# Small weight copies moved between engines and new planner ranks in a four-layer attention and gated-MLP kernel on one core

## The chip, the core and the metric

The kernel runs on one core of a Trainium2 chip. The metric is the device time of one execution in microseconds (us). The engines are TensorE (PE, its weight loads PEld), VectorE (DVE), ScalarE (ACT), GpSimd (POOL) and SyncE (SP), which issues the DMAs.

## The reference

One sequence of 2048 tokens with 576 features passes four layers: attention, MLP, attention, MLP, with the same weights both times. Each layer adds its result to its input.

```python
x = A_x
x = x + _A_ref(_layernorm(x, axis=-1), A_wqkv, A_wo)
x = x + _B_ref(_layernorm(x, axis=-1), B_w_gate, B_w_up, B_w_down)
x = x + _A_ref(_layernorm(x, axis=-1), A_wqkv, A_wo)
x = x + _B_ref(_layernorm(x, axis=-1), B_w_gate, B_w_up, B_w_down)
```

`_A_ref` has 32 heads of width 18. A token attends to 8 positions: itself and the 7 that lie 2, 4, ... 14 tokens before it; positions before the start are masked. The logits are scaled by 18 ** -0.5, a softmax over the 8 follows, then the weighted sum of values and the product with `wo` (576 x 576). `_B_ref` is `((x @ w_gate) * (x @ w_up)) @ w_down` with an inner width of 4608. Inputs and output are bfloat16.

## The kernel before

**Layout and loops.** Tokens lie in tiles of 128. Features are held on partitions in five blocks (four of 128, a tail of 64). The attention runs in jobs `j`: job 0 is tile 0 alone, job 1 tile 1 alone, and each later job is a chunk of two tiles; `seq` lists them. Jobs 0 to 4 belong to the first attention layer, job 5 is the first of the second. The MLP runs as `first_pair` (tiles 0 and 1), then `small(2)`, `small(3)`, `small(4)` (a chunk each), then `big` (four tiles at a time). In a `first_pair`, `small` or `big`, gate and up columns are multiplied in units (L1046, their 64-row tails in L1056), evacuated by ScalarE and VectorE (L1000 to L1005), and the down product follows in blocks (L1100, L1101). Projection units of a later attention job are put between the gate/up units where `IN_GU` says: in `{0: {3: [2]}}` job 2 goes in before unit 3 of `first_pair`.

**Preparing the weights.** `wqkv` is loaded raw (`wraw` for query and key, `wrav` for value) and copied into another order, one block `k` of 128 rows at a time, by `permute` (L351). For each `k` there are pieces by `t3`: 0 is query and 1 is key (128 x 512 each), 3 is the small rest of query and key (128 x 128), 2 and 4 are the same for value. Before, VectorE takes queries and most keys, ScalarE the keys of blocks 1 and 4 in two halves, and POOL the small pieces of blocks 0 to 3.

**An attention job.** `head` is the layer norm: statistics (L424, L426) on VectorE, the reciprocal root on ScalarE (L430, L431), the apply step on VectorE (L448) or ScalarE (L442, L443), then a transpose, either on PE (L460) with a ScalarE copy (L463), or by DMA (L453). `attention` runs one `head` before the projection (L551, for job 0 and part of job 1 L599), and one after it (its argument `ab` is 1) for the MLP input `xnT_B`. Between them: query x key products (`l1`, L744), sums over the head width (for jobs 0 and 1 on PE with the 0/1 matrix `Esel`, L760), softmax (L785, L798, L828 or L841), spreading the weights back over the partitions (`Bsel`, L863, or a DMA), value products (L912, L928; job 0 sums them on PE, L916 and L917), `wo` (L951; job 0 L479). Job 0 (`fast`) divides by the softmax sum only at the end: `total` makes the reciprocal (L834 to L836), `spread_z` and `rzs` spread it.

**Order of the work.** Every piece is registered with `op(engine, cost, function, r=, w=, prio=, after=)`: the data that it reads and writes, an estimated cost, and a rank (1 by default). `Plan.run` then simulates and emits the instructions; each engine runs its own in that order. Among all candidates it takes

```python
key = (t, o.prio, o.idx)
```

so the earliest estimated start wins, then the lowest rank, then the place in the list. `after` adds an order without data. Two details matter at the start: the identity matrix (`mk_ident`, L315 and L316), the zeroed halos (`mk_zero`, L334 and L336) and the selection matrices (`mk_sel`, L369 to L379: `Esel`, `Bsel`, `capb`) are all POOL pieces that can start at time 0; and before each PE piece the planner adds warm-up matmuls on the identity (`warm`, L967) for the idle time that it expects:

```python
self.warm(min(44, int(max(0, t - clock["PE"] - 100) / 100)))
```

This stops with the first gate/up unit (`bb`), whose pieces are chained in a fixed order on PE. The load of tile 2 waits for a small POOL memset (L307) that reads the small piece of block 0 (`wq3_0`); all loads of `wo` and of the MLP weights are queued behind it on SP.

Of the kernel before, what the change touches and what calls it, by code (L numbers as in the profile page):

```python
# [141 lines left out]
def kernel(  # L142
# [34 lines left out]
    KACT, VENG = (1, 4), ('POOL', 'POOL', 'ACT', 'ACT', 'ACT')  # L177
# [153 lines left out]
    def setup_b():  # L331
# [6 lines left out]
        def permute(k, t3, eng, prio, d0=0, nd=16, **kw):  # L338
            if t3 < 3:
                src = (wrav[:, k, :] if t3 == 2 else wraw[:, k, t3 * D:(t3 + 1) * D]).rearrange("p (h d) -> p d h", h=H)[:, d0:d0 + nd, :]  # L340
                dst = wqkv[:, k, t3 * 512 + d0 * H:t3 * 512 + (d0 + nd) * H].rearrange("p (d h) -> p d h", h=H)
                cost = {"DVE": 50 + 35 * nd, "ACT": 60 + 64 * nd, "POOL": 200 + 106 * nd}[eng]
            else:
                a, m = (0, 2) if t3 == 3 else (2, 1)
                src = (wrav[:, k, :] if a else wraw[:, k, :]).rearrange("p (t h d) -> p t d h", t=m, h=H)[:, :, 16:18, :]
                dst = wqkv[:, k, 1536 + 64 * a:1536 + 64 * (a + m)].rearrange("p (t d h) -> p t d h", t=m, h=H)
                cost = {"DVE": 80 + 75 * m, "ACT": 160 + 130 * m, "POOL": 250 + 180 * m}[eng]
            nm = "wrav" if t3 in (2, 4) else "wraw"
            rk = [f"{nm}{k}"] if k < KF else [f"{nm}t0", f"{nm}t{TL}"]
            cp = {"DVE": nc.vector.tensor_copy, "ACT": nc.scalar.copy, "POOL": nc.gpsimd.tensor_copy}[eng]  # L350
            return op(eng, cost, lambda: cp(dst, src), r=rk, w=[f"wq{t3}_{k}" + (f"_{d0}" if nd < 16 else "")], prio=prio, **kw)  # L351
# [34 lines left out]
        op("POOL", 3200, mk_sel, w=["sel"], prio=1)  # L386
# [11 lines left out]
        op("POOL", 0, swap, r=[f"wq{t}_{k}" for t in (0, 1, 3) for k in range(KT)],  # L398
# [20 lines left out]
    def head(src, keys, nst, dst, dkeys, prio, ab, on_pe, mg, first=None, then=None, dve=False):  # L419
# [19 lines left out]
        for i in range(nst):  # L439
# [4 lines left out]
            if dve:  # L444
# [4 lines left out]
                op("DVE", 420, apply_v, r=[keys[i], *mk, f"rstd{ab}"], w=[f"xn{ab}{i}"], prio=prio)  # L449
# [71 lines left out]
    LN1P = {2: 1.5, 3: 3, 4: 2, 5: 2.5, 6: 2.5, 7: 3, 8: 1, 1: 0.4}  # L521
    ATP = {1: 3, 2: 2.5, 3: 2.5, 4: 3, 5: 3, 6: 2}
    LPP = {1: 2.5, 2: 2, 3: 2.5, 4: 1.5, 5: 1.5, 6: 2}

    def attention(j, la, t0, nst, units=None):
# [5 lines left out]
        on_pe, pe_sum = j < 4, j < 2  # L531
        prio, mg = (1, 0) if fast else (ATP.get(j, 3), 200 if j < 5 else 1500)
# [5 lines left out]
        head(lambda i: xin[:, i0 + i, :], xin_k, nst, xnT_A, xk, LN1P.get(j, prio), 0, j < 3, mg, None,marks["evq"] if j == 1 else None, j < 3)  # L538
# [41 lines left out]
        def project(tag, au, bu, tl, ea, eb, dkeys):  # L580
# [35 lines left out]
            if fast:  # L616
# [14 lines left out]
                def values():  # L631
# [9 lines left out]
                    for cost, fn, w_, eng in eb[2:]:  # L641
                        op("ACT", cost, lambda fn=fn: fn(ub, 0), r=[kb, "uv"], w=w_, prio=0.5, free="unit", use=ub)
# [95 lines left out]
        for p_ in range(W // 2):  # L738
# [27 lines left out]
            op("DVE", 60 + 5.6 * n, l1, r=qk, w=[pk], prio=lprio, after=marks["xb1"] if j == 1 and p_ == 3 else None)  # L766
# [35 lines left out]
        else:  # L802
# [20 lines left out]
            op("DVE", 100 + 7 * n, gather_l, r=[f"part{jj}" for jj in range(4)] + ["cap"], w=["Lt"], prio=prio - 1, margin=2500 if j < 5 else 3000)  # L823
            op("DVE", 240 + 4.5 * n, soft1d, w=["Lt", "mx", "rg"], prio=prio - 1)
        if fast:
            late["values"]()
            rz = xn_[1][1]
            op("ACT", 170 + 1.8 * n, lambda: nc.scalar.activation(late["a_c"][:, 0:W * sq], late["Lt"][:, 0:W * sq], ACT.Exp),  # L828
               r=["Lt"], w=["ac"], prio=0)

# [25 lines left out]
        if on_pe:  # L856
# [15 lines left out]
            if fast:  # L872
                late["total"]()
                br = Bank()

                def spread_z():
                    for e in range(4):
                        for h_ in range(2):
                            nc.tensor.matmul(br()[:, e * sq:(e + 1) * sq], lhsT=Bsel[:, e].rearrange("p a b -> p (a b)"),
                                             rhs=rz[:, h_ * sq:(h_ + 1) * sq], start=(e == 0 and h_ == 0), stop=(h_ == 1), skip_group_check=True)  # L880
                op("PE", 350, spread_z, r=["zs", "xn11", "sel"], prio=0, **br.take())
                rzs = lambda: late["Lt"][:, 2 * P:2 * P + n]
                op("ACT", 300, lambda: nc.scalar.copy(rzs(), br()[:, 0:n]), r=[br.key, "Lt"], w=["rzs"], prio=0.5, **br.drop())
# [15 lines left out]
        for i_ in range(W):  # L899
# [21 lines left out]
            if fast:  # L921
# [3 lines left out]
                else:  # L925
                    marks["sum"] = op("PE", 330, gather, r=[pvk, "ident"], w=[bo[0].key, bo[1].key], prio=0)
            elif i_:
# [35 lines left out]
        head(lambda i: xs_f[:, i0 + i, :], fk, nst, xT, xTk, (1 if j > 1 else 0.5) if j < JSM + 2 else prio - 1, 1, j < 4, mg, None, None, j < 3)  # L963
# [366 lines left out]
    IN_GU, IN_D = {0: {3: [2]}, 2: {0: [3], 7: [4]}, 3: {2: [5], 12: [6]}}, {}  # L1330
# [41 lines left out]
```

## Time and profile before

| | us |
|---|---|
| median of 3 runs | 1048.6 (1048.55 to 1049.17) |
| the profiled execution | 1048.55 |
| its span in the profile | 1046.7 |
| PE busy | 1028.5 (98% of the span) |
| DVE busy | 723.0 (69%) |
| ACT busy | 446.3 (43%) |
| POOL busy | 14.5 (1%) |

A line of a timeline gives the start in us, the duration in us, the engine, the line of the kernel, the operation, output<-inputs, shapes, and how many instructions were merged (`x44`); in brackets the idle time before it and what ended that. Lines of the chain of waits give start, duration, engine, output and line. PE's ends are modelled, so pieces overlap by about 0.17 us.

### The profile page before, as it was taken

To read this page: it belongs to the slowest core of one execution; us is meant where nothing else is said; L and a number is where in the kernel's file an instruction comes from. 1 tells how busy PE (TensorE), PEld (TensorE's weight loads), DVE (VectorE), ACT (ScalarE), POOL (GpSimd) and SP (SyncE) were. 2 spreads that over 40 slices of the span, in tenths; PEclk is the share of its full clock that TensorE was granted. 3 is DMA by queue.
4 is the path that set the end of the run, shared out by engine and by line. 5 is a ranking of instruction groups with operands and counts; after the bars stand their busy time and mean duration, and the time that the engine had idled before them with its cause. 6 is when DMAs were issued, how large, how long until landed. Compare 5 with 4: busy or idle time off the path is not lost.

```text
span 1046.7 us, 19602 instructions
## 1 busy us (share of the span) xinstructions
PE 1028.5 (98%) x7898; PEld 595.9 (57%) x8016; DVE 723.0 (69%) x1366; ACT 446.3 (43%) x905; POOL 14.5 (1%) x54
## 2 busy tenths in 40 slices
PE   7999999999999999999999999999999999999998
PEld 6886886777765445554455544564455644554444
DVE  7896797889849886396766967579684796832211
ACT  4663763554645641354424443154531444214420
POOL 5000000000000000000000000000000000000000
PEclk9999999999999999999999999999999999999999
DMA  8918117454743805455143641635435352454212
GB/s 241 327 69 194 51 41 229 109 130 149 176 123 101 227 12 147 126 158 177 48 127 94 189 133 51 160 67 181 134 85 159 100 165 85 122 152 136 68 49 88
DMA packets 139834, 135.50 MB, mean 129 GB/s; under 512 B 43360, under 2 KB 137440, under 8 KB 139744
## 3 DMA queue, kind: packets, MB, share of 16 engines
q1 hardware_dynamic: 139744, 134.25, 45.0%
q8 instruction: 62, 1.02, 0.4%
q14 instruction: 28, 0.23, 0.1%
HBM read 114.49 MB, written 10.88 MB: 120 GB/s over the span
## 4 chain that ended last, share of the span: by engine, by line
PE 96%; issue 1%; DVE 1%; POOL 1%; ACT 0%; POOLq 0%; DVEq 0%
PE pu L1046 20%; PE pg L1046 18%; PE pg L1100 9%; PE pu L1100 8%; PE acct L1046 6%; PE pg L551 5%; PE pa L1046 4%; PE pu L551 4%; PE acct L1100 3%; PE pu L1056 3%; PE pg L1056 3%; PE pa L1100 2%; PE pg L1101 2%; PE pu L1101 2%; PE pa L951 1%
## 5 line engine op out<-in xcount | busy, mean ns | idle before, releaser
L1046 PEld LDWEIGHTS <-reg 128*128 128x128 bf16 x3072 | 277.5, 98 | 222.6 <-issue 24.2
L1046 PE MATMUL pu<-xnT_B,reg 128*128 128x512 bf16 (+2 forms) x1302 | 231.4, 316 | 1.3 <-issue 0.3
L1046 PE MATMUL pg<-xnT_B,reg 128*128 128x512 bf16 (+2 forms) x1204 | 220.4, 319 | 1.0 <-issue 0.2
L1100 PEld LDWEIGHTS <-reg 128*128 128x128 bf16 x864 | 84.4, 98 | 101.5
L1000 ACT CAST g_sb<-pu 128x512 bf16<-128x512 f32 x112 | 65.5, 588 | 126.3 <-PE pg L1056 66.2
L1003 DVE TENSOR_TENSOR reg<-reg,g_sb 128x512 bf16<-128x512 bf16 x144 | 59.7, 419 | 86.2 <-ACT reg L1002 76.6
L551 PEld LDWEIGHTS <-wqkv 128*128 128x128 bf16 (+1 forms) x1050 | 88.2, 97 | 34.0 <-issue 18.2
L744 DVE TENSOR_TENSOR prod<-qT,kT 128x2560 bf16<-128x2560 bf16 (+1 forms) x68 | 95.8, 1411 | 8.2 <-ACT kT L671 7.3
L912 DVE TENSOR_TENSOR prod<-vT,ab 128x1280 bf16<-128x1280 bf16 (+1 forms) x120 | 92.1, 776 | 0.0
L1000 ACT CAST g_sb<-pg 128x512 bf16<-128x512 f32 x112 | 65.8, 589 | 60.6 <-PE pu L1056 29.9
L928 DVE TENSOR_TENSOR qT<-qT,prod 128x1280 bf16<-128x1280 bf16 (+1 forms) x112 | 89.7, 801 | 2.5
L1101 PEld LDWEIGHTS <-reg 128*128 128x128 bf16 x864 | 84.9, 98 | 1.0
L430 ACT ACTIVATE rstd<-mv,eps_t 128x2 f32<-128x2 f32 (+1 forms) x33 | 9.8, 297 | 162.8 <-DVE mv L426 159.9
L1046 PE MATMUL acct<-xnT_B,reg 128*128 128x512 bf16 (+1 forms) x303 | 69.4, 354 | 0.5 <-issue 0.3
L551 PE MATMUL pg<-xnT_A,wqkv 128*128 128x256 bf16 (+1 forms) x500 | 69.6, 273 | 0.0
L1056 PE MATMUL pu<-xnT_B,reg 64*128 64x512 bf16 (+2 forms) x331 | 67.7, 316 | 0.1
L1101 PE MATMUL pu<-wd,reg 128*128 128x64 bf16 x336 | 64.8, 193 | 0.8
L1100 PE MATMUL pg<-wd,reg 128*128 128x512 bf16 x231 | 64.5, 380 | 0.0
L1056 PE MATMUL pg<-xnT_B,reg 64*128 64x512 bf16 (+2 forms) x305 | 62.8, 319 | 0.0
L551 PE MATMUL pu<-xnT_A,wqkv 128*128 128x256 bf16 (+1 forms) x410 | 59.1, 273 | 0.1
L1046 PE MATMUL pa<-xnT_B,reg 128*128 128x512 bf16 (+1 forms) x211 | 54.2, 376 | 0.6 <-issue 0.2
L1100 PE MATMUL pu<-wd,reg 128*128 128x512 bf16 x200 | 54.7, 380 | 0.0
(232 smaller groups left out, 1439.4 us busy)
## 6 DMA issues: line engine op xcount, KB each, us to landing
wd<-in_B_w_down_dram SPq DMA_DIRECT2D x152, 288.0 KB, 3.4
reg<-in_B_w_gate_dram SPq DMA_DIRECT2D x24, 768.0 KB, 4.8
reg<-in_B_w_up_dram SPq DMA_DIRECT2D x24, 768.0 KB, 6.3
reg<-in_B_w_down_dram SPq DMA_DIRECT2D x28, 288.0 KB, 3.3
s_dram<-s SPq DMA_DIRECT2D x13, 512.0 KB, 3.2
rg<-s_dram SPq DMA_DIRECT2D x52, 128.0 KB, 3.2
ab<-a_dram SPq DMA_DIRECT2D x52, 128.0 KB, 2.7
reg<-in_B_w_gate_dram SPq DMA_DIRECT2D x24, 96.0 KB, 5.6
```

The source lines that it names most:

```text
L430: nc.scalar.activation(rstd[:, 0:nst], mv[:, 0:nst, 1], ACT.Ln, bias=eps_t[:])
L551: nc.tensor.matmul(ring[use[p_]["slot"]][0:m, e * n:(e + 1) * n], lhsT=wqkv[r_, k, c0:c0 + m], rhs=xnT_A[r_, k, 0:n], start=start, stop=st ...
L744: nc.vector.tensor_tensor(late["prod"][lp(p_)][:, :, :, 0:n], q2, k2, op=ALU.mult)
L912: nc.vector.tensor_tensor(js(dst), js(vT[:, :, o0:o0 + n]), abw, op=ALU.mult)
L928: op("DVE", 60 + 3 * n, lambda tmp=tmp: nc.vector.tensor_tensor(oT[:, :, 0:n], oT[:, :, 0:n], tmp(), op=ALU.add), r=[pvk], w=ok, prio=prio)
L951: nc.tensor.matmul(b()[:, 0:HD], lhsT=oT[:, t, i * P:(i + 1) * P], rhs=wo_p[:, t, hh * HD:(hh + 1) * HD], start=(t == 0), stop=(t == KT - 1))
L1000: op("ACT", 590, lambda: nc.scalar.copy(g_sb[gs][:, 0:ul], bk(0)[:, 0:ul]), r=[keys[0]], w=[f"g{gs}"], prio=0, **fg)
L1003: op("DVE", 340, lambda: nc.vector.tensor_tensor(dst, dst, g_sb[gs][:, 0:ul], op=ALU.mult), r=[f"g{gs}"], w=[dk], prio=0)
L1046: nc.tensor.matmul(ring[use[q]["slot"]][:, e * n:(e + 1) * n], lhsT=w_[:, k], rhs=xT[:, k], start=(first and k == 0 and e == 0), stop=(las ...
L1056: nc.tensor.matmul(ring[use[q]["slot"]][:, e * n:(e + 1) * n], lhsT=w_[r_], rhs=xT[r_, KF], start=(fresh and e == 0), stop=not fresh, skip ...
L1100: nc.tensor.matmul(bank_of(i)[:], lhsT=lhs, rhs=wt[:, ft % 2, 0:512], start=first and not plus, stop=last_)
L1101: nc.tensor.matmul(tail_of(i), lhsT=lhs, rhs=wt[:, ft % 2, 512:D], start=(first and i == 0), stop=last_, skip_group_check=True)
```

## The change

- The small query and key pieces of all blocks are copied on VectorE. The key halves of blocks 1 and 3 go to ScalarE; of block 4, one half goes to ScalarE and one to POOL. The keys of blocks 0 and 2 are on VectorE.
- Planner costs: POOL copies are put lower, the VectorE apply step higher (620 for 420).
- `mk_sel` has rank 0.5 (was 1). The pool exchange `swap`, which holds no instruction, is listed on VectorE with rank 0 (was POOL, rank 1).
- The tables of ranks for jobs 1 to 8 change: `LN1P` (first layer norm), `ATP` (attention), `LPP` (query x key products). The first layer norm of job 1 goes from 0.4 to 1.6, that of job 2 from 1.5 to 2.5.
- The statistics of job 2's first layer norm come after the last gather of job 0 (`marks["sum"]`).
- The second layer norm transposes on PE only for job 1 (`LN2_PE = 2`, was `j < 4`), so those of jobs 2 and 3 go by DMA.
- In job 0 the exponential is listed ahead of the value weights, the 590 cost value copy comes after it, and `total`, `spread_z` and `rzs` are listed after the fourth value product.
- `gather_l` has a margin of 3000 (was 2500) for jobs under 5.
- `IN_GU` of `small(3)`: job 5 before unit 0 (was 2), job 6 before unit 13 (was 12).

```diff
-    KACT, VENG = (1, 4), ('POOL', 'POOL', 'ACT', 'ACT', 'ACT')
+    KENG = {1: ("ACT", "ACT"), 3: ("ACT", "ACT"), 4: ("ACT", "POOL")}
+    VENG = ('POOL', 'POOL', 'ACT', 'ACT', 'ACT')
+    LN1_PE, LN2_PE, ATT_PE, LN2_V, L1_LATE, MG, MGD = 3, 2, 4, 3, 3, 200, 3000
+    LN1_V = (0, 1, 2)
+    LN1_AFTER = {1: "evq", 2: "sum"}
...
-                cost = {"DVE": 50 + 35 * nd, "ACT": 60 + 64 * nd, "POOL": 200 + 106 * nd}[eng]
+                cost = {"DVE": 50 + 35 * nd, "ACT": 60 + 64 * nd, "POOL": 60 + 64 * nd}[eng]
...
-                cost = {"DVE": 80 + 75 * m, "ACT": 160 + 130 * m, "POOL": 250 + 180 * m}[eng]
+                cost = {"DVE": 80 + 75 * m, "ACT": 160 + 130 * m, "POOL": 160 + 120 * m}[eng]
...
-                if t3 == 1 and k in KACT:
-                    for d0 in (0, 8):
-                        permute(k, t3, "ACT", 1.5, d0, 8)
+                if t3 == 1 and k in KENG:
+                    for d0, e_ in zip((0, 8), KENG[k]):
+                        permute(k, t3, e_, 1.5, d0, 8)
                     pl.wr[f"wq1_{k}"] = [pl.wr[f"wq1_{k}_{d0}"][0] for d0 in (0, 8)]
                 else:
-                    permute(k, t3, "POOL" if t3 == 3 and k < KF else "DVE", 1.5)
+                    permute(k, t3, "DVE", 1.5)
...
-        op("POOL", 3200, mk_sel, w=["sel"], prio=1)
+        op("POOL", 3200, mk_sel, w=["sel"], prio=0.5)
...
-        op("POOL", 0, swap, r=[f"wq{t}_{k}" for t in (0, 1, 3) for k in range(KT)],
+        op("DVE", 0, swap, prio=0, r=[f"wq{t}_{k}" for t in (0, 1, 3) for k in range(KT)],
...
-                op("DVE", 420, apply_v, r=[keys[i], *mk, f"rstd{ab}"], w=[f"xn{ab}{i}"], prio=prio)
+                op("DVE", 620, apply_v, r=[keys[i], *mk, f"rstd{ab}"], w=[f"xn{ab}{i}"], prio=prio)
...
-    LN1P = {2: 1.5, 3: 3, 4: 2, 5: 2.5, 6: 2.5, 7: 3, 8: 1, 1: 0.4}
-    ATP = {1: 3, 2: 2.5, 3: 2.5, 4: 3, 5: 3, 6: 2}
-    LPP = {1: 2.5, 2: 2, 3: 2.5, 4: 1.5, 5: 1.5, 6: 2}
+    LN1P = {1: 1.6, 2: 2.5, 3: 2.5, 4: 2.5, 5: 2, 6: 3, 7: 3, 8: 2.5}
+    ATP = {1: 1.5, 2: 1.5, 3: 2, 4: 2, 5: 3, 6: 2.5}
+    LPP = {1: 2, 2: 1.5, 3: 1.5, 4: 1.5, 5: 1.5, 6: 1.5}
...
-        head(lambda i: xin[:, i0 + i, :], xin_k, nst, xnT_A, xk, LN1P.get(j, prio), 0, j < 3, mg, None,marks["evq"] if j == 1 else None, j < 3)
+        head(lambda i: xin[:, i0 + i, :], xin_k, nst, xnT_A, xk, LN1P.get(j, prio), 0, j < LN1_PE, mg, None if j == 1 else marks.get(LN1_AFTER.get(j)),
+             marks[LN1_AFTER[1]] if j == 1 else None, j in LN1_V)
...
-                        op("ACT", cost, lambda fn=fn: fn(ub, 0), r=[kb, "uv"], w=w_, prio=0.5, free="unit", use=ub)
+                        op("ACT", cost, lambda fn=fn: fn(ub, 0), r=[kb, "uv"], w=w_, prio=0.5, free="unit", use=ub,
+                           after=marks["exp"] if cost == 590 else None)
...
-            op("DVE", 100 + 7 * n, gather_l, ..., prio=prio - 1, margin=2500 if j < 5 else 3000)
+            op("DVE", 100 + 7 * n, gather_l, ..., prio=prio - 1, margin=MGD if j < 5 else 3000)
...
-            if fast:
-                late["total"]()
-                br = Bank()
...
+                if i_ == 3:
+                    late["total"]()
+                    br = Bank()
...
-        head(lambda i: xs_f[:, i0 + i, :], fk, nst, xT, xTk, (1 if j > 1 else 0.5) if j < JSM + 2 else prio - 1, 1, j < 4, mg, None, None, j < 3)
+        head(lambda i: xs_f[:, i0 + i, :], fk, nst, xT, xTk, (1 if j > 1 else 0.5) if j < JSM + 2 else prio - 1, 1, j < LN2_PE, mg, None, None, j < LN2_V)
...
-    IN_GU, IN_D = {0: {3: [2]}, 2: {0: [3], 7: [4]}, 3: {2: [5], 12: [6]}}, {}
+    IN_GU, IN_D = {0: {3: [2]}, 2: {0: [3], 7: [4]}, 3: {0: [5], 13: [6]}}, {}
```

More of the change, by code (lines that the diff above doesn't have):

```diff
@@ L926, in attention, with spread_z, rzs @@
                     marks["sum"] = op("PE", 330, gather, r=[pvk, "ident"], w=[bo[0].key, bo[1].key], prio=0)
+                if i_ == 3:
+                    late["total"]()
+                    br = Bank()
+                    def spread_z():
+                        for e in range(4):
+                            for h_ in range(2):
+                                nc.tensor.matmul(br()[:, e * sq:(e + 1) * sq], lhsT=Bsel[:, e].rearrange("p a b -> p (a b)"),
+                                                 rhs=rz[:, h_ * sq:(h_ + 1) * sq], start=(e == 0 and h_ == 0), stop=(h_ == 1), skip_group_check=True)
+                    op("PE", 350, spread_z, r=["zs", "xn11", "sel"], prio=0, **br.take())
+                    def rzs():
+                        return late["Lt"][:, 2 * P:2 * P + n]
+                    op("ACT", 300, lambda: nc.scalar.copy(rzs(), br()[:, 0:n]), r=[br.key, "Lt"], w=["rzs"], prio=0.5, **br.drop())
             elif i_:
```

24 lines of the change are left out of this document (9 added, 15 removed).

## The prediction

> **What bounds the kernel now.** I read the page (its span) first, then busy times by stretch, then the chain of waits through the first 42 us, then each engine's timeline there.
>
> ```profile
> span 1046.7 us, 19602 instructions
> ```
> ```profile
> 12.00:14.00 2.00, 2.00 (x23) 1.61 (x22) 0.12 (x1) 0.15 (x1) 2.00 (x9) 0.50 0.63 186
> 33.00:100.00 67.00, 66.55 (x903) 53.58 (x906) 53.91 (x112) 38.92 (x80) 0.00 (x0) 1.00 0.63 179
> 200.00:600.00 400.00, 396.88 (x2843) 228.49 (x2893) 301.43 (x570) 177.96 (x365) 0.00 (x0) 1.00 0.48 134
> ```
> The columns of the second fence are the stretch, its length, busy time of PE, PEld, DVE, ACT, POOL, then granted clock and DMA. From 33 us on TensorE is busy over 99% of the time at full clock. So after 33 us only matmul work taken off PE, or a new stall put on it, can move the end; before it, whatever brings the first gate/up matmul forward moves everything behind it. The profiled execution took 1048.55 us, 1.85 more than its span, and lies 0.05 under the median; the sum is made against it.
>
> ```profile
> 10.58 0.23 PE pu L599
> ...
> 11.88 0.21 PE pa L967 x2
> ...
> 13.27 0.22 PE pg L599
> ...
> 13.86 0.59 ACT qT L705
> ...
> 28.03 1.10 DVE xn L448 x4
> ...
> 29.85 0.75 DVE st L481 x2
> ...
> 33.61 1.02 PE pg L1046 x16
> ```
> This is the chain of waits (start, duration). Tile 0's projection ends at 13.86, and its chain reaches the first gate/up matmul at 33.61.
>
> ```profile
> 0.74 0.20 POOL L315 MEMSET ident<- 128x128 bf16 x1 [0.29 <-POOLq L1356]
> 1.01 0.29 POOL L316 TENSOR_SCALAR_AFFINE_SELECT ident<-ident 128x128 bf16<-128x128 bf16 x1
> ...
> 3.40 0.12 POOL L369 MEMSET Esel<- 128x32 bf16 x1
> ...
> 3.94 0.20 POOL L372 TENSOR_SCALAR_AFFINE_SELECT Esel<-Esel 128x32 bf16<-128x32 bf16 x1
> ...
> 5.11 2.50 POOL L374 TENSOR_SCALAR_AFFINE_SELECT Bsel<-Bsel 128x128 bf16<-128x128 bf16 x1
> ...
> 8.95 0.70 POOL L374 TENSOR_SCALAR_AFFINE_SELECT Bsel<-Bsel 128x128 bf16<-128x128 bf16 x1
> 9.60 0.18 POOL L376 MEMSET capb<- 128x112 bf16 x1
> ...
> 10.12 0.40 POOL L351 COPY wqkv<-wraw 128x128 bf16<-128x128 bf16 x1
> ```
> ```profile
> 1.36 4.24 PE L967 MATMUL pa<-ident 128*128 128x128 bf16 x44 [1.36 <-POOL ident L316]
> 5.44 0.44 PE L460 MATMUL pu<-ident,xn 128*128 128x128 bf16 x5
> ...
> 7.00 0.38 PE L599 MATMUL pg<-xnT_A,wqkv 128*128 128x128 bf16 x4 [0.39 <-ACT xnT_A L463]
> ```
> The first eight projection matmuls start at 7.00; the ninth needs the small copy that POOL makes only at 10.12, behind the selection matrices. That is the wait that the change takes away.
>
> **The change, part by part.**
>
> *Small copies to VectorE, key halves to ScalarE.* Four POOL copies leave the path. VectorE runs twelve copies where it ran nine, one large one fewer and four small ones more. This alone would let the projection go on at 7.00.
>
> *But the selection matrices get rank 0.5.* At time 0 the planner takes among ready pieces the lowest rank, and the identity keeps rank 1. So POOL builds Esel, Bsel and capb first and the identity after them, and the 44 warm-up matmuls (44 is the planner's cap, so their number stays) and tile 0's transposes, which read the identity, wait. The identity comes at 0.74 + 0.54 (memsets, 3.40 to 3.94) + 4 x (0.20 + S) + 0.52 (capb, 9.60 to 10.12) + 0.56 (0.74 to 1.30). S is one Bsel select: 0.29 as the identity's select of the same size, which ran with VectorE idle, or 0.65 (8.95 to 9.60). That gives 4.3 or 5.8; most of the selects will now run before VectorE's copies, so I take 4.7. A select that is held as the one at 5.11 was adds 2.2, which makes 8.0 the late end.
>
> ```profile
> 5.20 4.26 DVE L351 COPY wqkv<-wraw 128x512 bf16<-128x512 bf16 x8
> ```
> During the 2.50 us select VectorE ran these copies back to back. The Trainium skill, page "SBUF — State Buffer", section "SBUF: two separate sides", says that VectorE and GpSimd share a port pair as an exclusive lock: whichever starts first has it for its whole instruction, and the other blocks. By that rule more VectorE copies speak against this change, but one wait lasts one copy, about 0.6 us, and the sum below would hold; by the trace's row one select sat through some four copies, and the sum would be 2 us worse.
>
> From the identity: 4.08 of warm-up (1.36 to 5.44), 1.56 to the first projection matmul (5.44 to 7.00), four steps of 0.43 (10.58 to 11.88 is three), and 0.30 of tails.
>
> ```profile
> 8.63 1.21 ACT L351 COPY wqkv<-wraw 128x256 bf16<-128x256 bf16 x2 [1.68 <-DMA wraw<-in_A_wqkv_dram]
> ```
> The tails took 0.59 at a granted clock of 0.50; the clock fell after PE's idle time up to 10.58, which goes, so I halve it. ScalarE's last three key halves, 0.61 each, queue behind its copy of tile 0's transposes and end about 0.1 later than these steps. The projection ends at 4.7 + 7.75 = 12.45, against 13.86: **-1.4**. Bounds: 12.05 (-1.8), 13.5 (-0.35), and with a held select 15.7 (+1.8).
>
> *Tile 1's and chunk 2's normalisation ranked lower.*
> ```profile
> 16.71 0.63 DVE L448 TENSOR_SCALAR xn<-xf,mv,rstd 128x576 bf16<-128x576 bf16 x2
> 17.26 1.54 DVE L744 TENSOR_TENSOR prod<-qT,kT 128x1280 bf16<-128x1280 bf16 x2
> 18.73 0.81 DVE L424 BATCH_NORM_STATS2 st<-xf 128x6 f32<-128x288 bf16 x2
> ```
> ```profile
> 18.89 0.33 PE L760 MATMUL acct<-prod,Esel 128*32 128x64 bf16 x20
> ```
> Tile 1's apply (16.71 to 17.26) leaves the middle of tile 0's products: -0.55. Chunk 2's statistics now come after the last gather, so the maximum can start when PE is done (18.89 + 0.33 = 19.22) and not behind the statistics (18.73 + 0.81 = 19.54): -0.3. The apply is likely to land in that gap instead, 0.63 long, and I give half of it back: +0.3. **-0.55**, bounds -0.85 and 0.
>
> *After tile 0's values.*
> In the chain above chunk 2's apply (1.10 from 28.03) and then a product stand ahead of the two statistics at 29.85 that tile 0 waits for. Chunk 2 is now still at its own statistics there, in pieces of 0.4 (two take the 0.81 above), which block for less: **-0.5**, about half of the apply, bounds -1.1 and 0.
>
> *Sum and reciprocal.* They are listed later but keep rank 0, under the rank 1 of the value products, and depend on nothing new. The planner takes rank before place in the list, so I expect no move: 0. Even moved, all eight products and the reciprocal must be done on VectorE before tile 0's output, so the sum stays 0.
>
> *Second normalisation of chunks 2 and 3 by DMA.*
> ```profile
> 172.81 0.44 PE L460 MATMUL acct<-ident,xn 128*128 128x128 bf16 x5
> 173.09 0.38 PE L1100 MATMUL pu<-wd,hb 128*128 128x512 bf16 x1
> ...
> 175.82 1.04 PE L1046 MATMUL pg<-xnT_B,reg 128*128 128x256 bf16 x8
> ...
> 179.97 0.60 PE L551 MATMUL pg<-xnT_A,wqkv 128*128 128x256 bf16 x4
> ...
> 187.27 1.04 PE L1046 MATMUL pu<-xnT_B,reg 128*128 128x256 bf16 x8
> ```
> ```profile
> 172.20 0.42 ACT L443 ACTIVATE xn<-xf,nmr,rstd 128x64 bf16<-128x64 bf16 x1
> ```
> ```profile
> DMA to landing us min/median/max: 2.4/3.1/9.1
> ```
> Four such groups leave PE (two tiles each of chunks 2 and 3); the one at 172.81 holds PE for 0.28, until the next matmul at 173.09, in a stretch where PE is full: **-1.1**, bounds -1.1 and 0. The last row is all DMA transposes of this trace, from issue to landing. For chunk 3 the input is ready at 172.62, so the transposed tile is there at 176 to 182; PE uses it at 175.82 today. The move of job 5 to the front puts its 7.3 us of projection (179.97 to 187.27) ahead, to 183.1: covered, at 0. Without that cover it costs up to 5.9.
>
> The remaining ranks I take at 0: PE has no gap there for a rank to close. Sum: -1.4 - 0.55 - 0.5 - 1.1 = **-3.55**, so 1045.0 us.
>
> **The rivals.**
>
> *The identity is held.* If the identity's or a Bsel select falls among VectorE's copies and sits as the one at 5.11 did, the projection ends at 15.7 and the sum is +1.8 - 2.15 = -0.35: 1048.2. For it: the 2.50 us row, and three more copies. Against: of four Bsel selects only one was held. Chance 0.15.
>
> *Tile 1 does not keep up.*
> ```profile
> 55.05 0.69 ACT L463 COPY xnT_B<-pa 128x640 bf16<-128x640 bf16 x1 [0.59 <-PE pa L460]
> ```
> ```profile
> 56.07 0.27 PE L1056 MATMUL pg<-xnT_B,reg 64*128 64x256 bf16 x1
> ```
> Tile 1's input for the paired columns lands 0.3 us before PE uses it. Its chain on VectorE now also carries chunk 2's statistics, moved from 18.73. If it does not come forward with tile 0, the start's -2.45 is lost there and -1.1 stays: 1047.45. Against it: its own ranks are raised. Chance 0.10.
>
> *Slower: chunk 2's tile comes after tile 1's value products.*
> ```profile
> 40.75 0.49 DVE L912 TENSOR_TENSOR qT<-vT,ab 128x640 bf16<-128x640 bf16 x1 [0.55 <-ACT ab L671]
> ...
> 47.58 0.49 DVE L928 TENSOR_TENSOR qT<-qT,prod 128x640 bf16<-128x640 bf16 x1
> ```
> ```profile
> 41.12 0.60 PE L551 MATMUL pg<-xnT_A,wqkv 128*128 128x256 bf16 x4
> ```
> PE takes chunk 2's projection at 41.12 in a fixed order, with gate/up work queued behind. Chunk 2's normalisation now has rank 2.5 against 1.5 of tile 1's value products, which fill VectorE from 40.75 to 48.07. If chunk 2's apply is not issued before them (from there it decides), PE waits about their 7.3 us: 1045.0 + 7.3 = 1052.3. Against it: VectorE stands idle 0.55 before the first product and has other gaps before. Chance 0.13.
>
> **How the numbers follow.** Forecast 0.62, held identity 0.15, tile 1 0.10, chunk 2 late 0.13. A measurement tells 0.2%, 2.1 us, from no change: under 1046.5 is faster, over 1050.7 slower. The forecast is faster, the first two rivals are no change, the third is slower. The forecast's own bounds: all gains at their best, -1.8 - 0.85 - 1.1 - 1.1 = -4.85 or 1043.7; with the identity at 5.8, -2.5 or 1046.05. The range reaches to the two middle rivals and some of the price of the last, 1043.2 to 1049.5, with 0.5 us under the best sum for the ranks that I took at 0.
>
> **What would show it.** Right: POOL's first pieces are Esel and Bsel, the identity comes near 4.7, the first warm-up matmul right behind; the first q copy near 12.4; no small weight copy on POOL; the first gate/up matmul near 31.1; no PE transposes for the second normalisation near 97 and 173; PE over 99% busy from there on. Wrong: the identity still first at 0.74 (then more is gained); a select of over 2 us ahead of it; PE idle before chunk 2's projection or before the paired columns.

## The result, and the profile after: 0.4% slower

The changed kernel takes 1052.99 us (median of 8 runs, 1051.48 to 1054.0), the kernel before beside it 1048.57: ratio 1.0040 [1.0031, 1.0049]. The profiled execution took 1053.51 against 1048.55, so 4.96 more. The forecast was 1045.0 with a range to 1049.5: the time lies outside it, on the other side.

The page's span, and busy time by stretch, of the changed kernel (columns as in the prediction):

```profile
span 1051.7 us, 19595 instructions
```
```profile
12.00:14.00 2.00, 2.00 (x40) 1.79 (x38) 0.94 (x3) 1.03 (x3) 2.00 (x3) 1.00 1.06 220
33.00:100.00 67.00, 66.01 (x868) 52.50 (x873) 53.98 (x113) 36.59 (x76) 0.00 (x0) 1.00 0.66 177
200.00:600.00 400.00, 393.68 (x2807) 226.61 (x2853) 295.53 (x566) 179.11 (x368) 0.00 (x0) 0.99 0.48 129
```

At 12 to 14 us the clock is now 1.00 and not 0.50. From 33 to 100 TensorE is busy half a us less, and from 200 to 600 it is 3.2 us less at a mean clock of 0.99. The timeline of TensorE names the places:

```profile
31.89 1.10 PE L1056 MATMUL pg<-xnT_B,reg 128*128 128x128 bf16 x16
...
39.75 0.44 PE L1056 MATMUL pu<-xnT_B,reg 128*128 128x128 bf16 x5 [0.33 <-issue]
...
55.59 0.27 PE L1066 MATMUL pg<-xnT_B,reg 64*128 64x256 bf16 x1 [0.45 <-ACT xnT_B L467]
...
245.58 0.61 PE L1110 MATMUL pa<-wd,hb 128*128 128x512 bf16 x1 [3.12 <-DVE hb L1013]
```

Lines have moved by some ten (gate/up L1046 is L1056 here, down L1100 is L1110, query x key L744 is L750, value product L912 is L908, gate x up L1003 is L1013). TensorE stands 3.12 us before a down block of the third chunk, for a gate x up product of VectorE. Behind it, by stretch:

```profile
244.00:246.00 2.00, 0.42 (x2) 0.15 (x3) 1.97 (x4) 0.00 (x0) 0.00 (x0) 0.65 0.43 176
246.00:248.00 2.00, 1.78 (x10) 0.90 (x10) 2.00 (x4) 0.00 (x0) 0.00 (x0) 0.50 0.00 0
248.00:250.00 2.00, 2.00 (x11) 1.02 (x10) 1.17 (x3) 0.00 (x0) 0.00 (x0) 0.50 0.51 142
250.00:252.00 2.00, 2.00 (x14) 1.51 (x12) 1.97 (x5) 0.00 (x0) 0.00 (x0) 0.64 1.03 330
252.00:254.00 2.00, 2.00 (x23) 1.43 (x21) 1.02 (x2) 1.20 (x3) 0.00 (x0) 1.00 1.02 275
```

The granted clock falls to 0.50 and stays there until about 6 us after the gap, so the gap is paid nearly twice. VectorE's own timeline shows where the lateness began, 20 us earlier:

```profile
222.02 0.42 DVE L1013 TENSOR_TENSOR hb<-hb,g_sb 128x512 bf16<-128x512 bf16 x1 [4.09 <-ACT hb L1012]
227.99 1.56 DVE L908 TENSOR_TENSOR prod<-vT,ab 128x1280 bf16<-128x1280 bf16 x2 [5.54 <-DMA ab<-a_dram]
229.46 1.49 DVE L750 TENSOR_TENSOR prod<-qT,kT 128x2560 bf16<-128x2560 bf16 x1
...
245.10 0.42 DVE L1013 TENSOR_TENSOR hb<-hb,g_sb 128x512 bf16<-128x512 bf16 x1
```

Two value products of job 5 stand ahead of job 6's query x key products. Their spread weights `ab` are still in a DMA, and VectorE waits 5.54 us at them. Not all of this wait is lost, since most of the work behind was not ready either: ScalarE makes the next gate x up input only at 230.29, and the last key that the query x key products read here:

```profile
226.41 0.37 ACT L677 CAST kT<-pg 64x256 bf16<-64x256 f32 x1
```

So from 226.78 on ready work stood behind the two value products: 1.2 us of their wait and the 1.5 us that they run put the queue 2.7 us late (229.46 for 226.78). From 227.99 to the product that TensorE waits for, the last VectorE row above, VectorE has no idle time in which to catch up. In the kernel before the query x key products of job 6 came first, and all value products of job 5 behind them, from 238.47 on:

```profile
225.02 1.49 DVE L744 TENSOR_TENSOR prod<-qT,kT 128x2560 bf16<-128x2560 bf16 x1 [2.65 <-ACT kT L671]
```

Why `ab` is late, from SP's queue of the changed kernel:

```profile
216.37 0.34 SPq L882 DMA_DIRECT2D a_dram<-a_c  x1
217.86 3.14 SPq L302 DMA_DIRECT2D wd<-in_B_w_down_dram  x2
221.10 1.21 SPq L457 DMA_TRANSPOSE xnT_B<-xn  x1
222.39 1.96 SPq L885 DMA_DIRECT2D ab<-a_dram  x4
```

The weights left at 216.37, but the four loads that bring them back are issued only from 222.39, behind two loads of `wd` that take 3.14 us, 2.3 of it a wait, and a transpose that holds the queue 1.21 us. The place of the two value products in the queue fits a planner that expected `ab` earlier; its own estimate is not on record.

The ledger of the profiled executions, from the starts of the same pieces on TensorE's two timelines:

| up to | before | after | after - before |
|---|---|---|---|
| first gate/up matmul | 33.54 | 31.89 | -1.65 |
| job 2's projection | 41.12 | 40.03 | -1.09 |
| first down block (tiles 0, 1) | 82.18 | 81.71 | -0.47 |
| job 3's projection (chunk 2's gate/up) | 102.83 | 101.80 | -1.03 |
| third chunk's first TensorE piece | 175.82 | 174.23 | -1.59 |
| its seventh pair of down blocks | 237.78 | 236.20 | -1.58 |
| its eighth pair (the gap) | 243.94 | 245.58 | +1.64 |
| fourth chunk's first pair (the slow clock) | 254.47 | 258.69 | +4.22 |
| last matmul's end | 1042.96 | 1047.19 | +4.23 |
| span | 1046.7 | 1051.7 | +5.0 |

So the gap costs 3.22, the slow clock 2.58, and 0.77 is lost behind the last matmul. There the changed kernel has one instruction load more (DMA queues, 1047.2 to 1052; the kernel before has none in its last 4 us):

```profile
q14 instruction: 1, 0.01, 0.7%
```

Both kernels leave out a small piece of the work: by the code they issue 1136 of the 1152 down products of 512 columns. The loop of `small` reaches block 13 of 18 and its closing range starts at 16, so blocks 14 and 15 of the third and fourth chunk are missing in both. The difference between the two is not touched by it.

### The profile page after: what moved, and what is told of

It reads as the page before. It is cut to its first block, busy times and chain, and to the rows that moved or that the text cites. A ratio compares the mean times of both kernels' runs of the same rounds, so it can differ in the third digit from the quotient of the medians.

```text
span 1051.7 us, 19595 instructions
## 1 busy us (share of the span) xinstructions
PE 1029.2 (98%) x7890; PEld 595.9 (57%) x8008; DVE 724.3 (69%) x1369; ACT 443.3 (42%) x902; POOL 12.2 (1%) x51
## 3 DMA queue, kind: packets, MB, share of 16 engines
HBM read 114.49 MB, written 10.88 MB: 119 GB/s over the span
## 4 chain that ended last, share of the span: by engine, by line
PE 94%; DVE 2%; DMA 1%; issue 1%; SPq 1%; ACT 0%; DVEq 0%
PE pu L1056 19%; PE pg L1056 18%; PE pg L1110 9%; PE pu L1110 8%; PE pa L1056 6%; PE pg L556 5%; PE acct L1056 4%; PE pu L556 4%; PE pa L1110 3%; PE pu L1066 3%; PE pg L1066 2%; PE acct L1110 2%; PE pg L1111 2%; PE pu L1111 2%; PE acct L961 1%; PE pa L1066 1%
## 5 line engine op out<-in xcount | busy, mean ns | idle before, releaser
L1056 PEld LDWEIGHTS <-reg 128*128 128x128 bf16 x3072 | 278.7, 98 | 223.1 <-issue 24.9
L1056 PE MATMUL pu<-xnT_B,reg 128*128 128x512 bf16 (+2 forms) x1302 | 232.2, 317 | 1.7 <-issue 0.6
L1056 PE MATMUL pg<-xnT_B,reg 128*128 128x512 bf16 (+2 forms) x1204 | 220.5, 319 | 0.9 <-issue 0.2
L1110 PEld LDWEIGHTS <-reg 128*128 128x128 bf16 x864 | 84.5, 98 | 101.5
L1013 DVE TENSOR_TENSOR reg<-reg,g_sb 128x512 bf16<-128x512 bf16 x144 | 59.7, 419 | 86.1 <-ACT reg L1012 76.7
L750 DVE TENSOR_TENSOR prod<-qT,kT 128x2560 bf16<-128x2560 bf16 (+1 forms) x68 | 95.5, 1408 | 5.3 <-ACT kT L677 4.5
L908 DVE TENSOR_TENSOR prod<-vT,ab 128x1280 bf16<-128x1280 bf16 (+1 forms) x120 | 92.1, 777 | 5.7 <-DMA ab<-a_dram 5.5
L1056 PE MATMUL pa<-xnT_B,reg 128*128 128x512 bf16 (+1 forms) x303 | 69.4, 354 | 0.5 <-issue 0.3
L1110 PE MATMUL pg<-wd,reg 128*128 128x512 bf16 x231 | 64.4, 380 | 0.0
L1056 PE MATMUL acct<-xnT_B,reg 128*128 128x512 bf16 (+1 forms) x211 | 54.2, 375 | 0.6 <-issue 0.2
L1110 PE MATMUL pu<-wd,reg 128*128 128x512 bf16 x200 | 54.7, 380 | 0.0
```

Of the source, the lines that this page charges most:

```text
L750: nc.vector.tensor_tensor(late["prod"][lp(p_)][:, :, :, 0:n], q2, k2, op=ALU.mult)
L908: nc.vector.tensor_tensor(js(dst), js(vT[:, :, o0:o0 + n]), abw, op=ALU.mult)
L1013: op("DVE", 340, lambda: nc.vector.tensor_tensor(dst, dst, g_sb[gs][:, 0:ul], op=ALU.mult), r=[f"g{gs}"], w=[dk], prio=0)
L1056: nc.tensor.matmul(ring[use[q]["slot"]][:, e * n:(e + 1) * n], lhsT=w_[:, k], rhs=xT[:, k], start=(first and k == 0 and e == 0), stop=(las ...
L1110: nc.tensor.matmul(bank_of(i)[:], lhsT=lhs, rhs=wt[:, ft % 2, 0:512], start=first and not plus, stop=last_)
```

## The experiments

Theory A: the two value products at the head of VectorE's queue make the gap, and the gap makes the slow clock. Its rivals: job 5 in front is simply too much for VectorE there (B), the ranks alone do it (C), the DMA transposes on SP or the earlier start do it (D). Medians and ratios are against the kernel before on the same chip.

**1. A margin for the value products of all later jobs.**
```diff
-                   margin=0 if on_pe or i_ else 800 if j < 5 else 3500)
+                   margin=0 if on_pe or (i_ and j < 5) else 800 if j < 5 else 3500)
```


> The changed kernel, with the planner's margin of 3500 for all value products of jobs 5 and later, not only for the first one; the products of job 6's queries and keys then stand ahead of job 5's two early value products on VectorE. Theory A (VectorE stands 5.5 us before two value products whose spread weights are still in a DMA, its queue is late by that, PE then waits 3.12 us at 242.5 for a gate x up product, and the half clock after it costs about another 3.2): no wait of VectorE over 2 us near 222, no PE gap over 0.5 us near 242, granted clock 1.00 there, time 1053.0 - 6.3 = 1046.7. Rival B (job 5 in front gives VectorE too much work in this stretch, whatever its order): PE still waits over 2 us between 236 and 260, time above 1050.

1099.35 us, ratio 1.0467 [1.0452, 1.0481]. VectorE, then TensorE at the old place and at a new one:
```profile
228.14 1.49 DVE L750 TENSOR_TENSOR prod<-qT,kT 128x2560 bf16<-128x2560 bf16 x1 [4.37 <-ACT kT L677]
```
```profile
244.15 0.39 PE L1110 MATMUL pa<-wd,hb 128*128 128x512 bf16 x1 [0.36 <-DVE hb L1013]
...
311.92 1.86 PE L1056 MATMUL pu<-xnT_B,reg 128*128 128x512 bf16 x4 [5.93 <-ACT xn L447]
```
The query x key products come first and the gap falls from 3.12 to 0.36: the place is as theory A says, and B is out, since job 5 is still in front. Here the query x key products start as soon as their last key is there, and that alone, without the early value products, is soon enough for TensorE. The total was missed by 53 us: the same margin upset six later groups, where TensorE stands 5.8 to 7.6 us each (311.92 is the first).

**2. The places of jobs 5 and 6 as before.**
```diff
-    ... 3: {0: [5], 13: [6]}}, {}
+    ... 3: {2: [5], 12: [6]}}, {}
```


> The changed kernel with the place of the projections in the third chunk as before (job 5 before unit 2, job 6 before unit 12). Theory A with job 5's place as its trigger: the early value products no longer stand ahead, no PE gap over 0.5 us near 242, 1046.7 within 1. Rival C (the new ranks alone do it): the PE gap stays near 3 us, time about 1052 to 1053. Theory B expects the gap to go too.

1053.26, ratio 1.0040 [1.0026, 1.0054]; the 1046.7 is missed. The gap at 242 is gone (0.49 at 247.6), so C is out. But another has come:
```profile
177.35 0.96 PE L1056 MATMUL pg<-xnT_B,reg 128*128 128x256 bf16 x5 [2.86 <-DMA xnT_B<-xn]
```
```profile
176.00:178.00 2.00, 0.65 (x5) 0.91 0.92 248
178.00:180.00 2.00, 2.00 (x11) 0.50 1.02 327
```
(These columns are TensorE's busy time, clock and DMA.) Without job 5's projection in front, the third chunk's DMA transpose is uncovered; 2.86 us of standing brings the slow clock here too.

**3. Only ranks and places, on the kernel before.**
```diff
 (kernel before)
-    LN1P = {2: 1.5, 3: 3, 4: 2, 5: 2.5, 6: 2.5, 7: 3, 8: 1, 1: 0.4}
+    LN1P = {1: 1.6, 2: 2.5, 3: 2.5, 4: 2.5, 5: 2, 6: 3, 7: 3, 8: 2.5}
 (ATP, LPP and the places of jobs 5 and 6 likewise as in the change)
```


> The kernel before, with only the new places of jobs 5 and 6 and the three new tables of ranks. Theory A (these two together bring the softmax of job 5 early and put two value products first): PE gap near 3 us around 244 and half clock after it, time 1048.6 + 6.3 = 1054.9, a little less if the ranks help elsewhere. Rival D (the DMA transposes of the second normalisation crowd SP and make the spread weights late, or the earlier start shifts the real order against the plan): no such gap without them, 1048.6 within 1.

1059.76, ratio 1.0093 [1.0080, 1.0107], 5 us above the expectation. VectorE, then TensorE:
```profile
236.12 1.56 DVE L912 TENSOR_TENSOR prod<-vT,ab 128x1280 bf16<-128x1280 bf16 x2 [6.27 <-DMA ab<-a_dram]
```
```profile
32.83 3.04 PE L967 MATMUL pa<-ident 128*128 128x128 bf16 x27 [3.10 <-ACT xnT_A L463]
...
253.71 0.39 PE L1100 MATMUL acct<-wd,hb 128*128 128x512 bf16 x1 [3.84 <-DVE hb L1003]
```
The gap is there without the DMA transposes and without the new start: D is out as its cause. Most of the other 5 us are in the start: with the new ranks and the old start the planner put 27 warm-up matmuls (3.04 us) ahead of tile 0's transposes, TensorE stands 3.10 us before them, and the first gate/up matmul comes at 37.30 for 33.54.

**4. TensorE kept busy through the gap.**
```diff
+                    if (t0, b, i) == (4, 16, 0):
+                        for _ in range(14):
+                            nc.tensor.matmul(bank_of(0)[0:32, 0:512], lhsT=zer[:], rhs=reg[:, 0:512], start=False, stop=False, skip_group_check=True)
```


> The changed kernel with 14 matmuls of zeros (512 columns, about 0.21 us each, 3.0 us in all) added into an open sum just ahead of the block that waits at 242.5; they wait for nothing. If the half clock comes from PE's standing idle: the granted clock stays near 1.00 after 245.6, the gap's 3.1 us remains as time but the 3.2 us of slow matmuls goes, 1053.0 - 3.2 = 1049.8. If the slow matmuls after the gap have another cause: clock near 0.5 as before, 1053 or a little more.

1051.65, ratio 1.0019 [1.0011, 1.0028], 0.0021 under the changed kernel's, or 2.2 us.
```profile
243.64 3.20 PE L1110 MATMUL pa<-reg,zer 128*32 128x512 bf16 x14
247.08 0.39 PE L1115 MATMUL pa<-wd,hb 128*128 128x512 bf16 x1 [0.24 <-DVE hb L1015]
```
```profile
246.00:248.00 2.00, 1.76 (x11) 0.69 (x10) 2.00 (x4) 0.00 (x0) 0.00 (x0) 1.00 0.19 76
248.00:250.00 2.00, 2.00 (x18) 1.31 (x17) 2.00 (x4) 0.00 (x0) 0.00 (x0) 1.00 0.25 44
```
The clock stays at 1.00, and the eight down products behind take 2.06 us (247.08 to 249.14) where they took 3.83 (245.58 to 249.41). So the slow clock comes from the standing and not from the work behind it. About 0.8 of the expected 3.2 was lost in the start, whose first gate/up matmul came at 32.67 here and not at 31.89; whether the one memset more on POOL, for the zeros, did that was not tested.

**5. The margin for job 5 alone.**
```diff
-                   margin=0 if on_pe or i_ else 800 if j < 5 else 3500)
+                   margin=0 if on_pe or (i_ and j != 5) else 800 if j < 5 else 3500)
```


> The changed kernel with the margin of 3500 for all value products of job 5 alone (later jobs keep theirs; in the run with the margin for all of them PE stood 6 us in each later group of four tiles). Theory A: up to PE's wait at 242.5 nothing changes, then no gap over 0.5 us and no half clock, so the 1.58 us that the changed kernel is ahead of before at 236 stay; the end stays 0.77 later (measured from the last matmul). 1048.57 - 1.58 + 0.77 = 1047.8, against 1052.99 with the two products first. Rival: the planner's order of the later stages is upset again and they give it back, above 1050.

1050.68, ratio 1.0013 [1.0004, 1.0021], 2.9 above the expectation. Its only profile is of an execution of 2762.8 us and says nothing of the others. The seventh kernel, which differs only at the start, suggests where part of the 2.9 went: TensorE stands 1.69 us at 307.5, in the first group of four tiles, whose second DMA transpose is issued at 305.83 there and at 297.46 in the twelfth kernel. That job 5's products, held back, push this work is likely and was not shown.

**6. Places and both transposes as before.**
```diff
-    LN1_PE, LN2_PE, ... = 3, 2, ...
+    LN1_PE, LN2_PE, ... = 3, 4, ...
 (and the places of jobs 5 and 6 as in the second kernel)
```


> The changed kernel with both the places of jobs 5 and 6 and the second normalisation of chunks 2 and 3 on PE as before. With the places alone put back, PE stood 2.86 us at 174.5 before the first gate/up matmul of the third chunk. If that was the DMA transpose without job 5's projection as its cover: the gap goes, and with the ranks and the start of the changed kernel (0.47 ahead at 82 us) and an end 0.77 later the time is 1048.57 - 0.47 + 0.77 = 1048.9. If the ranks made that gap: it stays, about 1053.

1048.68, ratio 0.9998 [0.9989, 1.0006], near the expected 1048.9, and no gap over 0.45 us after 31 us: the DMA transposes without their cover made the gap of the second kernel. The nearness is in part luck, since the 0.77 at the end, which the sum took, did not come: against the kernel before beside it the time is 0.44 less, where 0.3 more was expected. The new start, ranks and all else of the change together are worth nothing that can be measured.

**7. The identity first, with the margin for job 5.**
```diff
-        op("POOL", 3200, mk_sel, w=["sel"], prio=0.5)
+        op("POOL", 3200, mk_sel, w=["sel"], prio=1)
```


> As the run with the margin for job 5 alone, and the selection matrices back at rank 1, so that POOL makes the identity first (0.74) and TensorE's warm-up starts at 1.36 and not at 4.21. If the identity limits the start: the first q copy comes from 12.97 to about 11 and the first gate/up matmul from 31.9 to about 30, time 1047.8 - 1.9 = 1045.9. If the last key copies limit it: first q copy at 12.5 or later, time within 0.5 of 1047.8. If VectorE's copies then hold the selection matrices (needed at 15): PE waits for them and the time is 1048 to 1050.

1052.57, ratio 1.0033 [1.0023, 1.0043]: slower, by none of the three ways. Its twelve runs lie from 1049.77 to 1054.96, which is wider than those of the kernel before (1048.09 to 1050.55). POOL, then TensorE:
```profile
12.37 4.50 POOL L355 COPY wqkv<-xl 128x64 bf16<-128x64 bf16 x7 [1.72 <-DMA xl<-in_A_wqkv_dram]
```
```profile
15.89 0.61 PE L604 MATMUL pg<-xnT_A,wqkv 128*128 128x128 bf16 x4 [3.20 <-POOL wqkv L355]
...
309.23 1.02 PE L1056 MATMUL pg<-xnT_B,reg 128*128 128x512 bf16 x4 [1.69 <-issue]
```
The warm-up starts at 1.37 and the first q copy comes at 11.61, 1.36 earlier than in the changed kernel: so far the first way is right, and the identity did limit the projection. But the value projection of tile 0 then waits 3.20 us for POOL's copies of the value weights, which start at 12.37 and not at 10.88, and the first gate/up matmul comes at 34.37. What the earlier identity would give without that wait was not run.

**8. The ranks as before, in the changed kernel.** The three tables of the third kernel's diff, put back.

> The changed kernel with the three tables of ranks as before. Theory A (it takes both the place of job 5 and the ranks to put the two value products first): no gap over 0.5 us near 242, chunk 3's DMA transpose still covered by job 5; the first gate/up matmul up to 1.05 us later than in the changed kernel, since tile 1's norm stands in tile 0's products again. 1048.57 - 0.6 - 1.1 + 0.77 = 1047.6. Rival (the place of job 5 alone does it): gap near 3 us, 1052 to 1053.

1066.77, ratio 1.0170 [1.0157, 1.0184], 19 above the expectation. No gap over 0.5 us between 72 and 321: theory A's half is right, it takes place and ranks together. But:
```profile
58.48 0.24 PE L766 MATMUL acct<-s,Esel 128*32 128x128 bf16 x4 [2.81 <-DVE s L760]
61.65 0.30 PE L766 MATMUL acct<-s,Esel 128*32 128x128 bf16 x4 [2.93 <-DVE s L760]
64.71 1.38 PE L961 MATMUL pa<-wo_p,qT 128*128 128x288 bf16 x5 [2.76 <-DVE qT L938]
```
With the old ranks and the new start, TensorE's sums for job 2 and tile 1's `wo` are ordered ahead of what VectorE can deliver, and the granted clock is 0.50 from 62 to 74. Ranks that cost nothing in one order cost 18 us in another.

**9 and 12. Job 6 before unit 12, and before unit 11; job 5 stays in front.**
```diff
-    ... 3: {0: [5], 13: [6]}}, {}
+    ... 3: {0: [5], 12: [6]}}, {}      (ninth kernel; 11 in the twelfth)
```


> The changed kernel with job 6 before unit 12 of the third chunk, as before, and job 5 still before unit 0. One unit earlier for job 6 and its query x key products stand ahead of job 5's value products on VectorE again. Theory A (the whole loss comes from that turn): no PE gap over 0.5 us near 242, chunk 3's DMA transposes still covered, 1048.57 - 1.58 (ahead at 236) + 0.77 (end) = 1047.8. Rival B (job 5 in front is too much for VectorE there): PE waits over 2 us between 236 and 260, over 1050.

> The changed kernel with job 6 before unit 11, job 5 before unit 0. The order of VectorE is right here too, and job 6 has two units more before its values are needed. Theory A: as with unit 12, 1047.8, or up to 0.5 less if work in the first group of four tiles was still late. If an earlier job 6 makes chunk 4's input late or loads VectorE: PE gap over 0.5 us between 210 and 260 and over 1049.

1048.12, ratio 0.9989 [0.9980, 0.9998], and 1048.19, ratio 0.9990 [0.9982, 0.9999]. VectorE and TensorE with 12, then VectorE with 11:
```profile
224.16 1.49 DVE L750 TENSOR_TENSOR prod<-qT,kT 128x2560 bf16<-128x2560 bf16 x1 [4.98 <-ACT kT L677]
```
```profile
173.06 0.38 PE L1110 MATMUL pg<-wd,hb 128*128 128x512 bf16 x1 [0.37 <-DMA wd<-in_B_w_down_dram]
...
243.94 0.39 PE L1110 MATMUL pa<-wd,hb 128*128 128x512 bf16 x1 [0.22 <-DVE hb L1013]
```
```profile
221.16 1.49 DVE L750 TENSOR_TENSOR prod<-qT,kT 128x2560 bf16<-128x2560 bf16 x1 [4.05 <-ACT kT L677]
```
One number, 12 for 13, takes back the whole loss: the query x key products stand first, the gap is 0.22, and the time is 5.3 under the changed kernel (each against the kernel before beside it) and 0.1% under the kernel before: 0.87 and 0.80 less, where 0.77 less was expected. These two are the best versions found. With 12, TensorE stands twice at 172.7 to 174.5 (0.37 and 0.31) for `wd` loads behind SP's transposes, which hold the queue 1.2 us each.

**10. Places as before, one chunk transposed on PE.**
```diff
-    LN1_PE, LN2_PE, ... = 3, 2, ...
+    LN1_PE, LN2_PE, ... = 3, 3, ...
 (and the places of jobs 5 and 6 as before)
```


> The changed kernel with the places of jobs 5 and 6 as before and the second normalisation by DMA for chunk 2 only, on PE for chunk 3. With both chunks on PE it took 1048.68. If a DMA transpose that is covered gives the whole of its two PE groups: 1048.68 - 0.56 = 1048.1, and no new gap before 103 us; and if the extra instruction load at the end comes with the shorter PE or ScalarE program, the end is 0.77 later again and the sum is 1048.9. If SP's 1.21 us per transpose delays a weight load: PE gap over 0.3 us near 100, and 1049 or more.

1053.44, ratio 1.0039 [1.0025, 1.0052]. The expectation has the chunks the wrong way round: `j < 3` puts job 2 (chunk 2) on PE and leaves chunk 3 to the DMA. Read so, it repeats the second kernel:
```profile
177.85 1.28 PE L1056 MATMUL pg<-xnT_B,reg 128*128 128x256 bf16 x8 [2.89 <-DMA xnT_B<-xn]
```
Chunk 3's transpose alone makes the gap of the second kernel. The end is 3.95 behind the last matmul, with no instruction load. What chunk 2's transpose alone would give was not run.

**11. Only the start, on the kernel before.**
```diff
 (kernel before)
-    KACT, VENG = (1, 4), ...
+    KENG = {1: ("ACT", "ACT"), 3: ("ACT", "ACT"), 4: ("ACT", "POOL")}
 (with the permute pieces, POOL costs, mk_sel at 0.5 and swap on DVE of the change)
```


> The kernel before with only the start of the change: small copies on VectorE, key halves on ScalarE and POOL, the POOL costs, the selection matrices at rank 0.5, the pool exchange on VectorE; ranks, places and transposes as before. If the start's gain is its own: first gate/up matmul at 33.54 - 1.4 + 1.05 (tile 1's and chunk 2's norms stay where they were) = 32.1 to 33.2, and 1048.57 - 0.4 to - 1.4 = 1047.2 to 1048.2. Rival: the planner's warm-up matmuls or tile 1's norm then fall in tile 0's path (as with the ranks alone, where 27 warm-up matmuls held it): first gate/up matmul at 34 or later, 1049 or more.

1049.29, ratio 1.0007 [0.9998, 1.0016]: the rival. TensorE:
```profile
12.62 0.83 PE L968 MATMUL pa<-ident 128*128 128x128 bf16 x12
...
34.48 1.21 PE L1047 MATMUL pg<-xnT_B,reg 128*128 128x128 bf16 x16 [0.57 <-ACT xnT_B L507]
```
Twelve warm-up matmuls fall ahead of the last block of tile 0's projection, so the first q copy comes at 13.82, no earlier than before (13.85). Behind it 0.94 us is lost: VectorE's division of tile 0's values starts at 28.36 for 27.14, and the first gate/up matmul comes at 34.48. With the old ranks the new start gives next to nothing, here and in the eighth kernel (33.38).

## Why the prediction was wrong

**What failed.** The step is the sentence "The remaining ranks I take at 0: PE has no gap there for a rank to close", and with it that the place of job 6 has no term in the sum at all (only job 5's is weighed). It looked for gaps that a rank could close and not for gaps that it could open. TensorE's order is fixed there, but VectorE's is the planner's; with job 6's projection one unit later its query x key products were ready later, and the planner put two value products of job 5 ahead of them. That it did so by too early an estimate of `ab` is argued from its rule and not read from the plan. In the trace `ab` came 11.6 us after it left (216.37 to 227.99), the two products ran first, and the query x key products started 2.7 us late. The gap that came of it is worth 3.22 + 2.58 = 5.8 us of the 8.5 between forecast and profile (1053.51 - 1045.0). The rest is 0.80 that the start gained less, 1.18 that was given back behind it, and 0.77 at the end. Six kernels show the cause: with both place and ranks the gap is there (third), with either alone it is not (second, eighth), and it goes when the two products are held back (first) or job 6 comes a unit or two earlier (ninth, twelfth).

**The identity and the selects: right.** They ran with VectorE idle, and the identity was there earlier than the 4.7 taken:
```profile
2.80 0.31 POOL L378 TENSOR_SCALAR_AFFINE_SELECT Bsel<-Bsel 128x128 bf16<-128x128 bf16 x1
...
3.86 0.29 POOL L320 TENSOR_SCALAR_AFFINE_SELECT ident<-ident 128x128 bf16<-128x128 bf16 x1
...
5.83 1.50 POOL L338 MEMSET vT<- 64x270 bf16 x2
```
All four `Bsel` selects took 0.31; the first rival (a held identity) did not occur. What was held is the zeroing behind them: 1.50 for a pair that takes 0.58 in the seventh kernel, where it ran at 2.41, before VectorE's copies.

**Tile 0's projection: too much hoped for.** ScalarE's first q copy of the changed kernel:
```profile
12.97 0.60 ACT L711 ACTIVATE qT<-pg 128x512 bf16<-128x512 f32 x1 [1.15 <-PE pu L604]
```
12.97 against 13.86 is -0.89 where -1.4 was forecast. The identity came 0.55 earlier than taken, and yet the end came 0.5 later. In the terms of the sum: the 44 warm-up matmuls took 4.66 (4.21 to 8.87) and not 4.08; from there to the projection it was 1.34 and not 1.56; the four steps took 2.33 (10.21 to 12.54) and not 1.72; the tails 0.43 and not 0.30. The steps were misread: what the prediction counted as three of 0.43 in the kernel before is two blocks of 0.50 (from 10.65 and 11.15) and two warm-up matmuls. A block takes 0.50 in the changed kernel too, and the planner put two warm-up matmuls ahead of the last block and two behind it (11.72 and 12.33). The prediction priced the 44 of the start and none of those.

**The rest of the start.** -1.65 at the first gate/up matmul against -2.45. Tile 1's normalisation out of tile 0's products gave -0.74 where -0.55 was forecast: the maximum starts at 17.94 for 19.57, and -0.89 of that is the projection's. Its apply landed ahead of the maximum (17.27), as foreseen. The -0.5 behind tile 0's values did not come: the division starts 1.71 earlier and the first gate/up matmul 1.65. Chunk 2's apply is gone from there, but `wo` comes only 1.43 earlier on TensorE (26.57), and a query x key product of tile 1 now stands between the two statistics. By the first down block 1.18 of it is given back: 0.28 because one of chunk 2's two transposes, which stood ahead of the first gate/up matmul (29.23), now stands behind it, and 0.33 and 0.45 in the two small gaps shown; the last 0.12 is not placed. The second of these is the rival "tile 1 does not keep up", true in part: 0.45 where it had the whole 2.45.

**Sum and reciprocal: right**, no move (they run from 19.4 to 20.8, ahead of the value products, as before). **Chunk 2's tile after tile 1's value products** (the slower rival) did not occur: its apply runs at 32.79, those products start at 39.79, and its projection at 40.03. That the rival's 1052.3 lies near the measured time is chance.

**The DMA transposes: right to the size, but not free.** Chunk 2 gains 0.56 (20.65 to 20.09 between the ledger's third and fourth row) and chunk 3 about 0.56, the -1.1 of the sum. The cover was judged rightly: without job 5 in front the price is 2.86 and the slow clock, and the second kernel takes 4.4 more than the sixth (each against the kernel before beside it), against "up to 5.9". What the sum lacked is the end: the load of instructions behind the last store. It is there in the changed kernel and the first, second, fourth, seventh, eighth, ninth and twelfth, which transpose both chunks by DMA, and not in the kernel before, the third, sixth, tenth and eleventh, which do not. (The fifth is not known.) That the transposes lengthen SP's program by just one load fits this and was not tested. So of the 1.1 some 0.77 goes back.

**The sum mended.** For the twelfth kernel, without the gap: -1.45 at the first gate/up matmul, -1.13 at the last matmul (1041.83 against 1042.96), and +0.77 at the end make -0.36 in the profiles, and -0.8 in the medians (1048.19 against 1048.99). Three of the four forecast gains are there in whole or in part, but what is left at the end is a quarter at most of the 3.55 that was taken.

## What to carry to other kernels

When an edit changes the inputs of a planner that lays out a queue, read what each engine's queue looks like at the moved piece, and not only the engine that sets the end: an instruction that waits for a DMA at the head of an in-order queue delays the ready work behind it, here by 2.7 us, and with no idle time in the queue the delay reached TensorE 16 us later. A rank or a place that "has no gap to close" can still open one; price it from what its piece would wait for if it came first, and from when the work behind it is ready. And single-edit gains don't add up where the edits meet in the order: the first gate/up matmul came at 34.48 with the start alone, at 37.30 with ranks and places alone, and at 31.89 with both.

## What the runs showed of the hardware

- Gaps of TensorE of 2.86 us (second kernel), 2.89 (tenth) and 3.12 (changed kernel) were enough for the granted clock to fall to 0.50; it came back to 1.00 some 4 us after the work resumed in the first two and some 6 us after in the third. Gaps of 1.39 us (eighth kernel) and 1.69 (seventh) left it at 1.00. With 14 matmuls of zeros in the gap (3.20 us) it stayed at 1.00. The Trainium skill, page "TensorE: Matmul & The Clock Gate", section "Part 1: The HAM clock gate", gives about 3.4 us of idle time before the half rate; here less was enough, by gaps that are read from modelled ends.
- VectorE stood 5.54 us at a value product, and the query x key products behind it, ready at 226.78, started only after it, at 229.46. The Trainium skill, page "PSUM — Partial Sum Buffer", section "Engine vs sequencer instructions", says that VectorE's queue is strictly first in, first out; the trace agrees.
- One DMA transpose holds SP's queue 1.21 us, three times the 0.39 of a `wd` load's issue (median); in the ninth kernel TensorE has two gaps of 0.37 and 0.31 for `wd` loads behind such transposes.
- One load of instructions at the very end, behind the last store's issue, goes with 0.77 us on the span (4.5 against 3.7 from the last matmul's end in the changed kernel and the one before); that it is the cause was not tested.
